# Linear attention and SwiGLU, forward and backward on one core: the key sum on another engine, and loads, stores and transposes around the attention loop at other times

## The chip, the cores and the metric

The kernel runs on one core of a Trainium2 chip. The core has five engines with queues of their own: TensorE (PE in the profile; its weight loads are PEld) multiplies matrices into PSUM, VectorE (DVE) and ScalarE (ACT) work on elements, GpSimd (POOL) does small vector work and issues DMAs, SyncE (SP) issues DMAs. ScalarE's queue can issue DMAs as well. The metric is the device time of one execution in microseconds. Before the change it is 819.78 us, the median of three runs (819.05 to 819.99). The change is measured against that kernel on the same chip.

## The reference

One pre-LayerNorm block with linear attention (32 heads of 20) and a SwiGLU FFN, and the gradients of its input and its five weights for a given `grad_out`. S = 2048 rows, D = 640, F = 1728, everything in bf16.

```python
phi = lambda t: jnp.where(t > 0, t + 1, jnp.exp(t)) + 1e-6
pq, pk = phi(q), phi(k)
kv = jnp.einsum("bhsd,bhse->bhde", pk, v)
z = jnp.einsum("bhsd->bhd", pk)                       # the sum of phi(k) over the rows
num = jnp.einsum("bhqd,bhde->bhqe", pq, kv)
den = jnp.einsum("bhqd,bhd->bhq", pq, z)[..., None] + 1e-6
o = num / den
attn = o.transpose(0, 2, 1, 3).reshape(B, S, D) @ wo

h  = x + attn(layernorm(x))
h2 = h + (silu(layernorm(h) @ w_gate) * (layernorm(h) @ w_up)) @ w_down
# outputs: h2, and the vector-Jacobian products of grad_out with x, wqkv, wo, w_gate, w_up, w_down
```

## The kernel before

The rows are 16 tiles of 128. The program has stages: LayerNorm and the projections of K and Q with phi; Y = xn^T phi(k) and from it the small matrices KVT and W2 (attention and `wo` folded into one 640 x 640 matrix); the attention loop, which forms h and its normalised form hn tile by tile; the FFN in four groups of columns with its weight gradients; then the rest of the backward pass. The change touches what lies from the end of the projections to the first FFN group.

Six pools matter. Each tag has so many slots, which tiles take one after another as they come free.

```python
psum   = tile_pool(bufs=4, space=PSUM)     # each tile two banks: [P, 2, 512] fp32
big    = tile_pool(bufs=5)                 # [P, 16, 640] bf16 and the like: dh2T, xn, xnT, pk, pqa, then pqsT, dm1, hn, hnT, dh2, ...
strips = tile_pool(bufs=4)                 # x_tm, wqk, wvo, then dm0, tzs, yk, dmst, m_s, dd, ...
wpool  = tile_pool(bufs=2)                 # wdT, wdT3, then the FFN weights wgu
work   = tile_pool(bufs=6)                 # rows: xr, zs, ...
fA: rr (used by phi) ; fpool takes its room when fA is closed
```

Gradient steps that don't depend on the attention ("dm" steps: `grad_out @ w_down^T` for two row tiles and one group of columns, ten matmuls and one copy out of PSUM by ScalarE) are kept in a generator and are put between other matmuls:

```python
def dm_steps():
    for g in (0, 1, 3):                       # 8 steps each; 448, 448 and 384 columns
        for t in range(0, ST, 2):
            ps = mm("ps_dm")
            dm_mm(ps, wdT3 if g == 3 else wdT, t, g)
            nc.scalar.copy(out=dst[:, :, :w], in_=ps[:, :, :w])
            if g == 3:
                nc.scalar.dma_start(out=scr_dm_v[:, t:t + 2, :], in_=dst[:, :, :w])
            yield
def dm(n): ...                                # the next n of the 24 steps
```

The head, the sum z and the stage of Y:

```python
warm(31)                                      # 128-wide matmuls of the identity
ln1_stats(0); ln1_centre(0, ...); copies(0, nc.scalar.copy)   # transposes of xn, copied to xnT
warm(8)
# ... cut: projections of K and Q for 16 tiles, phi(which, tiles) on VectorE ...

def z_sum():                                  # 32 matmuls: the rows of pk summed by a matrix of ones
    ps = mm("ps_z")
    for ci, (n0, n1) in enumerate(NCH):       # NCH = two halves of 320 columns
        for t in range(ST):
            q = t % 4 * H
            nc.tensor.matmul(ps[q:q + H, ci, :320], lhsT=ones[:, :H], rhs=pk[:, t, n0:n1],
                             start=(t < 4), stop=(t >= ST - 4))
    nc.scalar.copy(out=half(zs[0][:]), in_=row(ps))                 # z as a bf16 value and a bf16 rest
    nc.vector.tensor_tensor(out=half(zs[1][:]), in0=row(ps), in1=half(zs[0][:]), op=ALU.subtract)
    nc.vector.memset(KVT, 0.0)

for i in range(DT):                           # DT = 5
    ps = mm("ps_y")
    for ci, (n0, n1) in enumerate(NCH):
        for t in range(ST):
            nc.tensor.matmul(ps[:, ci, :320], lhsT=xn[:, t, i * P:(i + 1) * P], rhs=pk[:, t, n0:n1], ...)
        if (i, ci) == (0, 0):
            z_sum()
    nc.scalar.copy(out=half(Yt[:, i, :]), in_=row(ps))
    if i == 0:                                # z broadcast to all partitions: four matmuls ps_zb
        ps_z = mm("ps_zb")
        mm_row(ps_z, lambda k: ones32[:], lambda k, n0, n1: zs[k][:, n0:n1], 2)
        nc.scalar.copy(out=half(zb[:]), in_=row(ps_z))
        masks()
    if 0 < i < 4:
        dm(1)
dm(1)
for t in (0, 4):
    normalise(t)                              # four tiles of phi(q) divided by their denominators, on VectorE
    tr_pqs(t)                                 # their transposes by DMA, on SyncE's queue
# ... cut: kv_blocks (KVT, masked on VectorE), W2T and its transposes W2, with four dm steps between ...
for t in (8, 12):
    normalise(t)
    tr_pqs(t)
dm(2)
```

The attention loop, and the beginning of the FFN:

```python
for t in range(ST + 2):
    if t < ST:
        xr = xrs.pop(t)
        ps = mm("ps_a")
        mm_row(ps, lambda i: pqsT[:, i, t * P:(t + 1) * P], lambda i, n0, n1: W2[:, i, n0:n1], DT)
        nc.vector.tensor_tensor(out=half(xr[:]), in0=row(ps), in1=half(xr[:]), op=ALU.add)   # h1
        ln_stats(xr[:], mv[:, 0, :]); ln_rstd(mv, rstd2, t, 1)        # VectorE, then GpSimd
        dm(1)
    if t > 2:
        load_xr(t + 3)
    u = t - 2
    # ... cut ...
    nc.scalar.dma_start(out=scr_h1_v[:, u, :], in_=h1[:])
    nc.vector.tensor_scalar(out=hn[:, u, :], ...)
    nc.sync.dma_start_transpose(out=hnT[:, :, u * P:(u + 1) * P], in_=hn[:, u, :])

for c in range(4):
    nc.gpsimd.dma_start(out=dh2[:, c * 4:(c + 1) * 4, :], in_=go_v[...])      # the gradient
wgu = {0: load_wgu(0), 1: load_wgu(1)}
for g in range(4):
    for t in range(0, ST, 2):
        # pg and pu: twenty matmuls of hnT and wgu; g == 2 forms its dm step here (pdm)
        nc.scalar.activation(out=dg, in_=pg[:, :, :w], func=ACT.Sigmoid)
        # one more sigmoid and two copies on ScalarE, then seven products and sums on VectorE (m_s, dd);
        # dd transposed by DMA to stg, stg and m_s stored
    # dw: ps_dw from (dh2, m_s) and from (hn, dd), 16 row tiles each; the first one takes
    # the first 14 row tiles of both its parts ahead of the last two
```

Of the kernel before, what the change touches and what calls it, by code (L numbers as in the profile page):

```python
# [8 lines left out]
FP32 = mybir.dt.float32  # L9
# [6 lines left out]
P = 128  # L16
H = 32
# [3 lines left out]
def kernel(  # L21
# [216 lines left out]
    ones32 = const.tile([P, P], BF16, name="ones32")  # L238
    nc.vector.memset(ones32[:], 1.0 / H)
# [70 lines left out]
    def phi(which, t, n=2):  # L310
        e = (pk, pqa)[which][:, t:t + n, :]
        nc.vector.tensor_scalar(out=e, in0=e, scalar1=1.0, scalar2=1e-6, op0=ALU.min, op1=ALU.add)
        nc.vector.tensor_tensor(out=e, in0=e, in1=rr[:, 2 * which + t // 2 % 2, t % 2:t % 2 + n, :], op=ALU.add)
        if (t + n) % 4 == 0:
            sl = slice(t + n - 4, t + n)
            if which == 0:
                nc.sync.dma_start(out=scr_pk_v[:, sl, :], in_=pk[:, sl, :])
            else:
                nc.sync.dma_start(out=scr_pq_v[:, sl, :], in_=pqa[:, sl, :])
                nc.sync.dma_start(out=scr_xnT[sl].rearrange("t p k c -> p t k c"), in_=xnT[:, sl])  # L320

    PIECES = ((0, 3), (3, DT))

    with tc.manual_schedule(engines={EngineType.PE, EngineType.DVE, EngineType.Activation, EngineType.Pool}):
# [16 lines left out]
        warm(31)  # L341
# [16 lines left out]
        for t in range(2, ST):  # L358
# [14 lines left out]
            elif t == ST - 1:  # L373
                phi(0, t, 1)
                phi(1, t - 3)
                phi(1, t - 1)
# [8 lines left out]

    fA.close()
    fpool = wB.enter_context(tc.tile_pool(name="fpool", bufs=6))
# [33 lines left out]
    def masks():  # L421
        tc.keep_in_program_order(nc.gpsimd.memset(mask[:], 1.0))
        for c0, n, p0 in ((0, 6, 0), (120, 2, 88)):
            m = mask[:, c0:c0 + n * Dh]
            for sign in (1, -1):
                tc.keep_in_program_order(nc.gpsimd.affine_select(
                    out=m, in_=m, pattern=[[-sign * Dh, n], [0, Dh]], compare_op=ALU.is_ge, fill=0.0,
                    base=-p0 if sign > 0 else p0 + Dh - 1, channel_multiplier=sign))
# [10 lines left out]
    def normalise(t):  # L439
# [7 lines left out]
        nc.vector.reciprocal(out=rall[:, t:t + 4, :], in_=den[:])  # L447
        nc.vector.tensor_tensor(out=hb4(pq), in0=hb4(pq), in1=bc4(rall[:, t:t + 4, :]), op=ALU.mult)

    def tr_pqs(t):  # L450
        for tt in range(t, t + 4):
# [9 lines left out]
    with tc.manual_schedule(engines={EngineType.PE, EngineType.DVE, EngineType.SP}):  # L461
        yk = strips.tile([P, DT * D + HG * P], BF16, name="yk", tag="S")
        Yt = yk[:, :DT * D].rearrange("p (k n) -> p k n", k=DT)
        KVT = yk[:, DT * D:].rearrange("p (j c) -> p j c", j=HG)
        zs = [wk("zs"), wk("zl")]

        def z_sum():
            ps = mm("ps_z")
            for ci, (n0, n1) in enumerate(NCH):
                for t in range(ST):  # L470
                    q = t % 4 * H
                    nc.tensor.matmul(ps[q:q + H, ci, :320], lhsT=ones[:, :H], rhs=pk[:, t, n0:n1],
                                     start=(t < 4), stop=(t >= ST - 4))
            nc.scalar.copy(out=half(zs[0][:]), in_=row(ps))
            nc.vector.tensor_tensor(out=half(zs[1][:]), in0=row(ps), in1=half(zs[0][:]), op=ALU.subtract)
            nc.vector.memset(KVT, 0.0)

        for i in range(DT):
            ps = mm("ps_y")
            for ci, (n0, n1) in enumerate(NCH):  # L480
# [3 lines left out]
                if (i, ci) == (0, 0):  # L484
                    z_sum()
            nc.scalar.copy(out=half(Yt[:, i, :]), in_=row(ps))
            if i == 0:
                ps_z = mm("ps_zb")
                mm_row(ps_z, lambda k: ones32[:], lambda k, n0, n1: zs[k][:, n0:n1], 2)
                nc.scalar.copy(out=half(zb[:]), in_=row(ps_z))  # L490
                masks()
# [3 lines left out]
        for t in (0, 4):  # L495
            normalise(t)
            tr_pqs(t)
# [14 lines left out]

        kv_blocks(KVT, "ps_kvt", lambda i, a, b: wv[:, i, a:b], lambda i, a, b: Yt[:, i, a:b])

# [3 lines left out]
        for i in range(DT):  # L518
# [5 lines left out]
            nc.sync.dma_start_transpose(out=W2[:, :, i * P:(i + 1) * P], in_=W2T[:, i, :])  # L524
        for t in (8, 12):
            normalise(t)
            tr_pqs(t)
        dm(2)

        hn = big.tile([P, ST, D], BF16, name="hn", tag="B")  # L530
        hnT = big.tile([P, DT, S], BF16, name="hnT", tag="B")
        h1s = {}
        for t in range(ST + 2):
# [10 lines left out]
            if t > 2:  # L544
                load_xr(t + 3)
# [488 lines left out]
```

## Time and profile before

| What | us |
|---|---|
| Median of three runs (lowest, highest) | 819.78 (819.05, 819.99) |
| Span of the profiled execution, first to last instruction | 817.2 |
| First matmul of Y (ps_y) | 54.6 |
| First matmul of the attention loop (ps_a) | 98.1 |
| First matmul of the FFN (pg) | 146.4 |
| First matmul of its first weight gradient (ps_dw) | 176.7 |
| Last matmul ends | 813.8 |

Granted TensorE clock over the span: 1.000. The first column of a line in the order of time is the start in microseconds from the first instruction, the second its length or, for several of a kind, the length of the stretch; then come the engine, the line of the program, the operation, output and inputs, and a count. An entry in brackets is time for which the engine stood idle before it, and what ended the wait. Matmuls overlap, and the profile models their ends: what one costs in a row is seen from start to start. ScalarE's queue (ACTq) and SyncE's queue (SPq) show the issue of DMAs, not the transfers.

### The profile page before, as it was taken

What the parts mean: (1) busy time and instruction counts of PE and PEld (TensorE: products, weight loads), DVE (VectorE), ACT (ScalarE), POOL (GpSimd) and SP (SyncE); (2) the same over time, 40 slices, a digit from 0 to 9 for tenths busy, and PEclk for the clock granted to TensorE, in tenths of its full rate; (3) what the DMA queues carried; (4) which work ended last, traced back from release to release, by engine and by line L of the source; (5) the groups of instructions that cost most, each with busy time, mean ns of one, the idle gap of its engine ahead of it and who ended that gap; (6) DMA issues with size and microseconds to landing.
All of it is one profiled execution on the core that took longest, in us unless ns stands there. A gap on an engine that the chain in (4) does not pass through costs nothing.

```text
span 817.2 us, 13969 instructions
## 1 busy us (share of the span) xinstructions
PE 811.2 (99%) x5534; PEld 521.7 (64%) x5534; DVE 442.5 (54%) x849; ACT 288.2 (35%) x405; POOL 192.8 (24%) x350
## 2 busy tenths in 40 slices
PE   9999999999999999999999999999999999999998
PEld 7776666545555555555566677777777777777675
DVE  7878787791087018800760147787892366631212
ACT  6982422760184126400841122322312133322010
POOL 3420022223312412221125501211220121112330
PEclk9999999999999999999999999999999999999999
DMA  9994789999559987993498757976499999999942
GB/s 302 192 360 86 169 202 277 258 221 214 132 137 222 205 201 153 206 268 81 107 252 165 259 134 219 216 213 167 114 239 165 175 159 181 174 212 251 273 132 72
DMA packets 278321, 158.61 MB, mean 194 GB/s; under 512 B 235052, under 2 KB 264877, under 8 KB 278256
## 3 DMA queue, kind: packets, MB, share of 16 engines
q1 hardware_dynamic: 251696, 82.12, 52.7%
q0 software_dynamic: 17744, 64.45, 26.0%
q10 hardware_dynamic: 8816, 11.16, 4.5%
q8 instruction: 43, 0.70, 0.4%
q14 instruction: 22, 0.18, 0.1%
HBM read 47.68 MB, written 53.66 MB: 124 GB/s over the span
## 4 chain that ended last, share of the span: by engine, by line
PE 94%; DVE 4%; DMA 1%; ACT 0%; issue 0%; ACTq 0%; DVEq 0%
PE ps_dw L652 21%; PE ps_dhn L109 14%; PE ps_dxn L904 8%; PE ps_o L966 7%; PE ps_kq L302 5%; PE ps_dwqk L109 5%; PE pg L583 5%; PE pu L588 5%; PE ps_dm L396 5%; PE ps_y L482 3%; PE ps_gt L711 3%; PE ps_dp L109 3%; PE ps_dk L109 3%; PE ps_a L109 3%; PE pdm L396 2%; DVE m_s L613 1%
## 5 line engine op out<-in xcount | busy, mean ns | idle before, releaser
L109 PE MATMUL ps_dhn<-wgT,cols 128*128 128x320 bf16 x864 | 119.5, 299 | 0.0
L652 PE MATMUL ps_dw<-dd,hn 128*128 128x448 bf16 (+1 forms) x640 | 118.8, 346 | 0.0
L109 PEld LDWEIGHTS <-cols 128*128 128x128 bf16 x864 | 84.5, 98 | 32.9
L652 PEld LDWEIGHTS <-hn 128*128 128x128 bf16 x640 | 62.6, 98 | 54.2
L654 DVE CAST dwev<-ps_dw 128x896 bf16<-128x896 f32 (+3 forms) x12 | 10.9, 906 | 122.9 <-PE ps_dw L652 122.9
L654 ACT CAST dwev<-ps_dw 128x896 bf16<-128x896 f32 (+1 forms) x20 | 17.6, 878 | 159.4 <-PE ps_dw L652 151.5
L617 POOL DMA_DIRECT2D scr_dT<-stg x64 | 34.7, 542 | 164.2 <-DMA stg<-dd 159.4
L147 DVE CUSTOM_DVE_ANT_0 lb_a<-lb_dy,hn 128x640 bf16<-128x640 bf16 x32 | 26.5, 829 | 75.5 <-ACT lb_dy L145 75.5
L583 PE MATMUL pg<-wgu,hnT 128*128 128x448 bf16 (+1 forms) x320 | 63.6, 346 | 0.0
L588 PE MATMUL pu<-wgu,hnT 128*128 128x448 bf16 (+1 forms) x320 | 63.6, 346 | 0.0
L652 PE MATMUL ps_dw<-m_s,dh 128*128 128x448 bf16 (+1 forms) x320 | 60.7, 346 | 0.6 <-DVE m_s L613 0.4
L966 PE MATMUL ps_o<-wd,mT 128*128 128x320 bf16 (+3 forms) x462 | 61.1, 295 | 0.0
L904 PEld LDWEIGHTS <-ring 128*128 128x128 bf16 x480 | 47.0, 98 | 18.2
L966 PEld LDWEIGHTS <-mT 128*128 128x128 bf16 (+1 forms) x462 | 41.8, 97 | 17.4 <-issue 2.6
L904 PE MATMUL ps_dxn<-wqkvT,ring 128*128 128x320 bf16 x320 | 51.3, 299 | 0.0
L652 PEld LDWEIGHTS <-dh 128*128 128x128 bf16 x320 | 31.3, 98 | 28.0 <-issue 1.1
L588 PEld LDWEIGHTS <-hnT 128*128 128x128 bf16 x320 | 31.3, 98 | 27.1
L583 PEld LDWEIGHTS <-hnT 128*128 128x128 bf16 x320 | 31.3, 98 | 27.0
L396 PE MATMUL ps_dm<-wdT,dh2T 128*128 128x448 bf16 (+1 forms) x240 | 47.0, 344 | 0.0
L396 PEld LDWEIGHTS <-dh2T 128*128 128x128 bf16 x320 | 31.0, 98 | 24.8
L302 PE MATMUL ps_kq<-wqk,xnT 128*128 128x320 bf16 x320 | 46.3, 299 | 0.0
L145 ACT ACTIVATE lb_dy<-ps_dhn,rstd 128x640 bf16<-128x640 f32 x16 | 12.7, 793 | 87.1 <-PE ps_dhn L109 87.1
(166 smaller groups left out, 1277.4 us busy)
## 6 DMA issues: line engine op xcount, KB each, us to landing
scr_dT<-stg POOLq DMA_DIRECT2D x48, 224.0 KB, 3.2
cols<-scr_dT POOLq DMA_DIRECT2D x6, 1728.0 KB, 8.3
scr_m<-m_s POOLq DMA_DIRECT2D x12, 448.0 KB, 4.5
cols<-scr_dT ACTq DMA_DIRECT2D x2, 1728.0 KB, 10.2
out_dram<-dwev POOLq DMA_DIRECT2D x30, 112.0 KB, 2.2
scr_dT<-stg POOLq DMA_DIRECT2D x16, 192.0 KB, 2.9
scr_pk<-pk SPq DMA_DIRECT2D x4, 640.0 KB, 8.2
scr_xnT<-xnT SPq DMA_DIRECT2D x4, 640.0 KB, 8.2
```

What stands on the lines that cost most here:

```text
L109: nc.tensor.matmul(ps[:, ci, :320], lhsT=lhs(k), rhs=rhs(k, *NCH[ci]), start=(start and k == 0), stop=(stop and k == n - 1))
L147: nc.vector.tensor_tensor_reduce(out=a[:], in0=dy[:], in1=xhat, scale=1.0, scalar=0.0, op0=ALU.mult, op1=ALU.add, accum_out=sums[:, 1:2])
L302: nc.tensor.matmul(ps[:, ci, :320], lhsT=xnT[:, t, k, :], rhs=wqk[:, k, w0 + n0:w0 + n1], start=(k == 0), stop=(k == DT - 1))
L396: nc.tensor.matmul(ps[:, c, :w], lhsT=dh2T[:, kt, (t + c) * P:(t + c + 1) * P], rhs=wdT[:, kt, o:o + w], start=(kt == 0), stop=(kt == DT - 1))
L482: nc.tensor.matmul(ps[:, ci, :320], lhsT=xn[:, t, i * P:(i + 1) * P], rhs=pk[:, t, n0:n1], start=(t == 0), stop=(t == ST - 1))
L583: nc.tensor.matmul(pg[:, c, :w], lhsT=hnT[:, kt, (t + c) * P:(t + c + 1) * P], rhs=wg[:, kt, 0:w], start=(kt == 0), stop=(kt == DT - 1))
L588: nc.tensor.matmul(pu[:, c, :w], lhsT=hnT[:, kt, (t + c) * P:(t + c + 1) * P], rhs=wg[:, kt, w:2 * w], start=(kt == 0), stop=(kt == DT - 1))
L617: nc.gpsimd.dma_start(out=scr_dT[t + c, :, KO[g]:KO[g] + GK[g], :], in_=stg[:, :GK[g], :])
L652: nc.tensor.matmul(ps[:, c, :w], lhsT=lhs(t), rhs=rhs(t), start=(t == 0), stop=(t == ST - 1))
L654: last = copy(out=ev[:, :len(parts), :w], in_=ps[:, :len(parts), :w])
L904: nc.tensor.matmul(ps[:, ci, :320], lhsT=lhs[:, i, :], rhs=rhs[:, i, n0:n1], start=(k == 0 and i == 0), stop=(k == 2 and i == DT - 1))
L966: nc.tensor.matmul(po(t, ci), lhsT=mTs[t // 4][r, t % 4, j, :], rhs=wd[r, j, n0:n1], start=(t, ci) not in opened, stop=last)
```

## The change

It does several things at once between the projections and the FFN. z is summed by VectorE in fp32 rather than by matmuls with ones, ahead of the last four tiles of phi(q); only its broadcast stays on TensorE, later in the stage. Twelve of the 24 dm steps come ahead of the attention loop, where nine did; one of the others stands inside the first row of the loop. Transposes of the last normalised tiles and of hn are spread over the loop, h1 is stored through GpSimd's queue instead of ScalarE's, and a one-column sigmoid in the loop makes ScalarE load its table there. The gradient and the second FFN weights are loaded only after the first sigmoid of the second pair of tiles of the first FFN group. The aim is to take work off TensorE and to have the other engines' queues free where the FFN begins. The diff, with cuts:

```diff
-    ones32 = const.tile([P, P], BF16, name="ones32")
-    nc.vector.memset(ones32[:], 1.0 / H)
...
-        warm(31)
+        warm(37)
...
             elif t == ST - 1:
-                phi(0, t, 1)
-                phi(1, t - 3)
-                phi(1, t - 1)
+                last_phi = phi(0, t, 1)
...
-    def normalise(t):
+    def norm_den(t):
... (the first four operations) ...
+    def norm_mul(t):
... (the product) ...
-    with tc.manual_schedule(engines={EngineType.PE, EngineType.DVE, EngineType.SP}):
+    with tc.manual_schedule(engines={EngineType.PE, EngineType.DVE, EngineType.SP, EngineType.Pool}):
+        z2 = tzs[:, 4:8].rearrange("p t d -> p (t d)").bitcast(FP32)
+        zf = z2[:, :D]
+        tok2 = pk.rearrange("p (t two) d -> p t (two d)", two=2)
+        with tc.issue_after(last_phi):
+            nc.vector.tensor_tensor(out=z2, in0=tok2[:, 0], in1=tok2[:, 1], op=ALU.add)
+        for t in range(2, ST // 2):
+            nc.vector.tensor_tensor(out=z2, in0=z2, in1=tok2[:, t], op=ALU.add)
+        nc.vector.tensor_tensor(out=zf, in0=zf, in1=z2[:, D:], op=ALU.add)
         zs = [wk("zs"), wk("zl")]
-        def z_sum(): ... (whole, as shown above)
+        nc.vector.tensor_copy(out=zs[0][:], in_=zf)
+        nc.vector.tensor_tensor(out=zs[1][:], in0=zf, in1=zs[0][:], op=ALU.subtract)
+        for t in (ST - 4, ST - 2):
+            phi(1, t)
+        nc.vector.memset(KVT, 0.0)
+        masks()
+        def z_bcast():
+            ps = mm("ps_zb")
+            mm_row(ps, lambda k: ones[:], lambda k, n0, n1: zs[k][:, n0:n1], 2)
+            nc.scalar.copy(out=half(zb[:]), in_=row(ps))
...
-                if (i, ci) == (0, 0):
-                    z_sum()
+                if (i, ci) == (2, 1):
+                    z_bcast()
... (ps_zb after i == 0 is gone) ...
-        for t in (0, 4):
-            normalise(t)
-            tr_pqs(t)
+        norm_den(0)
+        norm_mul(0)
+        tr_pqs(0)
+        norm_den(4)
...
         kv_blocks(KVT, "ps_kvt", ...)
+        norm_mul(4)
...
+        tr_pqs(4)
         for t in (8, 12):
-            normalise(t)
-            tr_pqs(t)
-        dm(2)
+            norm_den(t)
+            norm_mul(t)
+            if t < 12:
+                tr_pqs(t)
+        dm(5)
...
-                mm_row(ps, lambda i: pqsT[...], lambda i, n0, n1: W2[:, i, n0:n1], DT)
+                for ci, (n0, n1) in enumerate(NCH):
+                    for i in range(DT):
+                        nc.tensor.matmul(ps[:, ci, :320], lhsT=pqsT[...], rhs=W2[:, i, n0:n1], ...)
+                    if t == 0 and ci == 0:
+                        dm(1)
...
-                dm(1)
+                if t > 0 and t % 4 != 3:
+                    dm(1)
+            while h1_todo and h1_todo[0][0] < t:
+                v, h1 = h1_todo.pop(0)
+                nc.gpsimd.dma_start(out=scr_h1_v[:, v, :], in_=h1[:])
             if t > 2:
                 load_xr(t + 3)
+            if t < 4:
+                tr_pqs(12 + t, 1)
+            if t == 3:
+                hnT = big.tile([P, DT, S], BF16, name="hnT", tag="B")
...
             if u == 0:
+                nc.scalar.activation(out=small.tile([P, 1], FP32, ...)[:], in_=h1s[0][1][:, 0, 0:1], func=ACT.Sigmoid)
...
-            nc.scalar.dma_start(out=scr_h1_v[:, u, :], in_=h1[:])
...
-            nc.sync.dma_start_transpose(out=hnT[:, :, u * P:(u + 1) * P], in_=hn[:, u, :])
+            hnT_todo.append(u)
+            for v in hnT_todo[:0 if t < 4 else 2]:
+                hnT_todo.pop(0)
+                nc.sync.dma_start_transpose(out=hnT[:, :, v * P:(v + 1) * P], in_=hn[:, v, :])
+    fA.close()                                   # moved here from ahead of the stage of Y
+    fpool = wB.enter_context(tc.tile_pool(name="fpool", bufs=6))
...
-        wgu = {0: load_wgu(0), 1: load_wgu(1)}
+        wgu = {0: load_wgu(0)}                   # and the four loads of dh2 became the generator load_dh2()
...
+                sig = nc.scalar.activation(out=dg, in_=pg[:, :, :w], func=ACT.Sigmoid)
+                if g == 0 and t == 2:
+                    wait_for(sig, load_dh2())
+                    wgu[1] = load_wgu(1)
```

## The prediction

> **What bounds the kernel now.** I read the page's busy table first, then the groups, then the order of time on TensorE and the chain that ended last, stage by stage. From the page:
>
> ```profile
> PE 811.2 (99%) x5534; PEld 521.7 (64%) x5534; DVE 442.5 (54%) x849; ACT 288.2 (35%) x405; POOL 192.8 (24%) x350
> ```
>
> TensorE is busy for 811.2 of 817.2 us. Matmul ends are modelled, so a busy share alone doesn't say that it runs at full rate; spacings do. In the view in order of time, ten 448-wide matmuls take 1.89 us (189 ns from start to start) and ten 320-wide take 1.36 us (136 ns), and these spacings hold almost everywhere. So TensorE is the bound, and only two things shorten the kernel: fewer matmuls, or the few places where its spacing breaks. From the groups, kept apart by shape, the matmuls that this change removes:
>
> ```profile
> L472 PE MATMUL ps_z<-pk,ones 128*32 128x320 bf16 x32 | 1.3, 300 | 0.0
> ```
>
> And from the order of time around the end of the K and Q projections, the first break (start, length, engine, line, count):
>
> ```profile
> 94.33 3.94 PE L396 MATMUL ps_dm<-wdT,dh2T 128*128 128x448 bf16 x20
> ...
> 98.11 0.84 PE L109 MATMUL ps_a<-wvo,pqsT 128*128 128x320 bf16 x5
> ...
> 99.14 0.85 PE L109 MATMUL ps_a<-wvo,pqsT 128*128 128x320 bf16 x5 [0.19 <-DMA wvo<-wvo]
> ```
>
> Five 320-wide matmuls from 98.11 end their issue at 98.11 + 5 x 0.136 = 98.79, the next start at 99.14: 0.35 us lost to the last transpose of W2. The second break is at the first dw of the FFN, from TensorE's order of time:
>
> ```profile
> 176.71 2.43 PE L652 MATMUL ps_dw<-m_s,dh 128*128 128x448 bf16 x12
> 179.56 4.25 PE L652 MATMUL ps_dw<-m_s,dh 128*128 128x448 bf16 x20 [0.42 <-DVE m_s L613]
> 183.65 6.59 PE L652 MATMUL ps_dw<-dd,hn 128*128 128x448 bf16 x34
> ```
>
> 176.71 + 12 x 0.189 = 178.98, so 0.58 lost before 179.56; 179.56 + 20 x 0.189 = 183.34, so 0.31 lost before 183.65. Both times VectorE hadn't written m_s. Why it was late is read from the chain that ended last (start, length, what):
>
> ```profile
> 149.31 0.16 ACTq L554
> 149.48 0.03 issue
> 149.51 1.28 ACT L604
> 150.80 0.92 ACT dd L604
> ...
> 153.36 0.64 DVE m_s L613
> ...
> 182.23 0.62 DVE m_s L613
> 182.86 0.04 issue
> 182.90 7.16 PE ps_dw L652 x37
> ```
>
> ScalarE's queue was held by the last h1 stores (L554) until 149.48, then it loaded the sigmoid table, 1.28 us, and VectorE could begin only at 153.36. In this stage VectorE needs about as long for a pair of tiles (seven products of 0.54 us, 3.8 us) as TensorE (two times 1.89 us), so it never makes up a late start. A last gap lies at the head: 31 warm-up matmuls from 1.42, 107 ns apart, end at 4.73, and the transposes start at 5.35. All breaks after the head together are about 2 us of 817, so the change has little room.
>
> [...]here spacings fall from 107 to 56 ns at about 6.5 us. [...]the trace before has none from SBUF, but its fp32 add out of PSUM (xr, 640 elements) takes 818 ns[...]; the group of L604 shows the same 1283 ns.
>
> **The change part by part.**
>
> z on VectorE. It removes the 32 ones-matmuls: in the chain they stand for 1.20 us (56.92 to 58.12), and the sixteen ps_y matmuls right after them take 2.28 instead of 2.17 us. Saved on the path: 1.3 us. Added on VectorE after the last phi of K (ends 55.5): seven fp32 adds of 1280 elements,[...] one of 640 (0.82), a cast of 640 (about 0.5) and a difference (0.82). With about 30 ns between dependent operations that is 12.9 us, an estimate, so the two z halves stand at 68.4. The broadcast (4 matmuls, 0.54 us, as before) now comes after the third ps_y row: 54.74 + 3 x 4.35 + 1.89 = 69.7. It should not wait, with 1.3 us to spare.
>
> VectorE afterwards. The last two phi of Q (2.6 us) and the memset (0.4) follow, to 71.4; zb is ready at about 71.5, where it was 61.75. Each group of four tiles costs 1.49 + 2.82 + 0.23 + 0.95 = 5.5 us for the denominators and 2.83 for the product, 8.4 with gaps. First group to 79.9, second denominators to 85.5. TensorE reaches ps_kvt at 84.6 and ends it at 86.0 (a dm step of 1.89 follows), the masks are done at 86.9: no wait. Three more products and two denominators end at about 106.6, where it was 104.5.
>
> Twelve dm steps ahead. They were nine, so the loop starts 3 x 1.9 - 1.3 = 4.4 us later, at 98.1 + 4.4 = 102.5. W2's transposes landed at 99.1 before, so the 0.35 us break goes. Moved steps cost nothing: all 24 remain. The first ps_a row ends at about 105.8 (0.68 + 1.9 + 0.68, as a dm step now stands in its middle) and VectorE picks it up at 106.6; four PSUM buffers cover that. In the loop TensorE needs (4 x 1.36 + 3 x 1.62)/4 = 2.6 us per tile with the narrow steps, VectorE 0.82 + 0.89 + 0.21 + 0.40 plus gaps, 2.45. It holds, narrowly.
>
> h1 stores on GpSimd, table early. ScalarE's queue is free of the sixteen stores and has its table since about 108. TensorE starts the FFN at 146.44 - 1.3 - 0.35 = 144.8, the first pg is complete 2.1 us later, and ScalarE starts at about 147.0 instead of 150.80. VectorE starts 2.56 us after that, at about 149.5 instead of 153.36: 3.8 us earlier, while TensorE is 1.65 us earlier. The slack of 2.2 us exceeds the 0.89 us lost at the first dw, so both waits go.
>
> Loads and transposes. The gradient load and the second weight pair start after the third sigmoid at about 151, and so leave the queue to the hn transposes. They were issued at 145 to 151 and land in some 10 us; the first dw needs the gradient at 175. Hidden before and after.
>
> Head. Six more warm-up matmuls fill the 0.62 us gap, but nothing gets ready sooner: the transposes wait for xn. The order of the built program also puts the mask's memset (the identity's memset of 128 columns takes 0.20 us there, this one has 160) ahead of the identity; then 37 x 0.107 from about 1.6 ends at 5.55, 0.2 later than now.[...] I book +0.1.
>
> Sum: -1.3 - 0.35 - 0.89 + 0.1 = -2.4 us, so 819.8 - 2.4 = 817.4.
>
> **The rivals.**
> 1. VectorE becomes the bound between 55 and 110. For it: 12.9 us of new work where it had 1.2, on an engine that the loop uses to 94%. Against: it stood idle for 7.7 us ahead of the kvt masks, which the new work may fill. If the adds cost 20% more, z is late by about 1 us and TensorE waits for zb or the masks: 818 to 819. If the loop falls behind as well, the FFN start loses what the table gave: 820.
> 2. The later loads are missed. The fourth gradient piece stands in GpSimd's queue behind two stores of transposed tiles, which wait for SyncE's transposes; those stood back until 163 before. If that repeats, the piece is issued at about 167 and, at up to 10 us to landing, comes by 177, just when it is needed (175 + 12 x 0.19). A miss costs 1 to 5 us: 818 to 822.
> 3. The m_s waits stay, because something else than the table holds ScalarE (the slot of dd, a store). Then 0.9 is not won: 818.3.
>
> **Range and chances.** The sum is three small terms, each read off to about 0.1 us; the three runs before spread over 0.94 us. Rival 3 and the head give a high side of about 1 us, rivals 1 and 2 (together perhaps one in six) up to 3 more. An earlier clock is the only gain beyond the sum. I predict 817.4 us, with 816.3 to 819.2 for 8 in 10. Two per cent are 16.4 us, far more than any break can return or any rival costs: faster 0.01, within 2% 0.98, slower 0.01.
>
> **What would show it.** Right: no ps_z; 50 ps_dm matmuls back to back ahead of ps_a with no DMA wait; ps_dw of the first group without an m_s wait; first m_s product at about 149.5; TensorE's first pg at about 144.8; zl ready ahead of ps_zb. Wrong: ps_zb or ps_kvt's masks waiting for VectorE, ps_dw waiting for a DMA of dh, pg for hnT, or a first kq later than 6.9. A time above 819.5 would refute the sum, one below 816 would mean that I overlooked a loss.

## The result, and the profile after

The changed kernel takes 822.36 us (median of 6 runs, 821.62 to 822.93); the kernel before, in the same measurements, 819.67 (818.49 to 820.91). The ratio is 1.0032 with a 95% interval of 1.0019 to 1.0045: the change costs 2.7 us, where the prediction had it win 2.4. The gains that the prediction listed did come. A new wait in the attention loop, with a stretch of half clock behind it, took more than all of them.

From the page of the kernel after, the busy table and the costliest group that now waits (busy, mean ns | idle before, releaser). The 32 ones-matmuls of z are gone and six warm-up matmuls are new (5508 instead of 5534), yet TensorE's busy time is longer (812.0 for 811.2 us), which points to matmuls that ran slower:

```profile
PE 812.0 (99%) x5508; PEld 522.5 (64%) x5508; DVE 453.0 (55%) x857; ACT 288.1 (35%) x405; POOL 200.4 (24%) x366
...
L390 PE MATMUL ps_dm<-wdT,dh2T 128*128 128x448 bf16 (+1 forms) x240 | 47.5, 348 | 3.2 <-DVE xr L549 3.2
```

TensorE in order of time, kernel after (start, length, engine, line, count, idle time before it and its releaser):

```profile
93.33 9.62 PE L390 MATMUL ps_dm<-wdT,dh2T 128*128 128x448 bf16 x50
102.79 0.84 PE L545 MATMUL ps_a<-wvo,pqsT 128*128 128x320 bf16 x5
103.47 2.05 PE L390 MATMUL ps_dm<-wdT,dh2T 128*128 128x448 bf16 x10
...
133.42 2.88 PE L545 MATMUL ps_a<-wvo,pqsT 128*128 128x320 bf16 x20
139.47 2.73 PE L390 MATMUL ps_dm<-wdT,dh2T 128*128 128x384 bf16 x10 [3.17 <-DVE xr L549]
142.00 2.30 PE L545 MATMUL ps_a<-wvo,pqsT 128*128 128x320 bf16 x10
144.13 1.79 PE L390 MATMUL ps_dm<-wdT,dh2T 128*128 128x384 bf16 x10
...
150.10 2.06 PE L612 MATMUL pg<-wgu,hnT 128*128 128x448 bf16 x10
...
180.37 2.43 PE L684 MATMUL ps_dw<-m_s,dh 128*128 128x448 bf16 x12
183.22 3.96 PE L684 MATMUL ps_dw<-m_s,dh 128*128 128x448 bf16 x20 [0.42 <-DMA dh<-in_grad_out_dram]
```

The reader sees three of the announced signs: fifty dm matmuls in a row, no wait for W2 at the first ps_a (102.79 + 5 x 0.136 = 103.47), no wait for m_s at ps_dw. And two that were named as signs of being wrong: 3.17 us of idle TensorE at 139.47, after which ten 384-wide matmuls take 2.73 us instead of 1.79, and a wait of ps_dw for the gradient (180.37 + 12 x 0.189 = 182.64, so 0.58 lost). The first pg comes at 150.10; it was announced for 144.8.

Two windows of 5 us from the same trace (length, then busy time of TensorE, its weight loads, VectorE, ScalarE and GpSimd, granted clock, DMA share, GB/s). From 140.16 on the clock is at half for 3.41 us:

```profile
135.00:140.00 5.00, 1.83 (x14) 1.13 (x13) 1.37 (x3) 0.80 (x1) 0.00 (x0) 1.00 0.99 245
140.00:145.00 5.00, 5.00 (x24) 2.77 (x23) 4.83 (x13) 0.80 (x1) 2.92 (x6) 0.66 0.99 289
```

What VectorE waited for, from its order of time:

```profile
130.91 0.82 DVE L549 TENSOR_TENSOR xr<-ps_a,xr 128x640 bf16<-128x640 f32 x1 [1.73 <-DMA xr<-in_A_x_dram]
...
138.59 0.82 DVE L549 TENSOR_TENSOR xr<-ps_a,xr 128x640 bf16<-128x640 f32 x1 [5.38 <-DMA xr<-in_A_x_dram]
```

It is the load of x (xr) of tile 10, the residual that is added to the attention's row. Until it lands, the PSUM buffers aren't freed and TensorE stops. The chain of waits of the kernel after, at this place, names the load as the longest piece:

```profile
130.63 7.84 DMA xr<-in_A_x_dram
...
138.59 0.84 DVE xr L549
139.43 0.04 issue
139.47 2.73 PE ps_dm L390 x10
```

Why it came so late shows in SyncE's queue, which issues one transfer after another. Kernel after (start, issue time, line, count):

```profile
98.34 15.37 SPq L449 DMA_TRANSPOSE pqsT<-pqa  x11
...
126.45 0.52 SPq L456 DMA_DIRECT2D xr<-in_A_x_dram  x1
127.07 0.61 SPq L185 DMA_DIRECT2D wgu<-in_B_w_gate_dram  x1
127.73 0.74 SPq L186 DMA_DIRECT2D wgu<-in_B_w_up_dram  x1
128.56 1.98 SPq L581 DMA_TRANSPOSE hnT<-hn  x1
130.63 0.86 SPq L456 DMA_DIRECT2D xr<-in_A_x_dram  x1
```

and the same queue of the kernel before, where the load of tile 10 is the one at 123.94:

```profile
97.75 13.00 SPq L452 DMA_TRANSPOSE pqsT<-pqa  x8
...
122.21 0.38 SPq L185 DMA_DIRECT2D wgu<-in_B_w_gate_dram  x1
122.69 1.21 SPq L557 DMA_TRANSPOSE hnT<-hn  x1
123.94 0.56 SPq L459 DMA_DIRECT2D xr<-in_A_x_dram  x1
124.56 0.48 SPq L186 DMA_DIRECT2D wgu<-in_B_w_up_dram  x1
```

The queue differs in three ways. As z comes later, normalise does, and twelve pqsT transposes instead of eight stand behind W2's, at 1.2 us of issue or more each. The loop's hnT transposes start late and then come two a step. And both wgu loads of the first FFN group (0.56 MB each), which the diff doesn't touch, now stand together, just in front of tile 10's load. It is issued 6.7 us later than before and takes 7.84 us to land instead of 4.6, while VectorE wants it only 1.5 us later (133.21 for 131.73). The twelve transposes aren't what puts the two halves of wgu there: with z left on TensorE eight stand behind W2's, and the halves fall together all the same (below, the rest alone).

Had the kernel before shown this risk? Yes. In its loop the transfer engines are as full (DMA share 1.15 from 125 to 140), and its tile 11 was already late, only not by enough to reach TensorE. VectorE of the kernel before:

```profile
134.99 0.82 DVE L538 TENSOR_TENSOR xr<-ps_a,xr 128x640 bf16<-128x640 f32 x1 [0.96 <-DMA xr<-in_A_x_dram]
```

That load had taken 7.80 us from issue to landing, behind the second wgu load.

### The profile page after: what moved, and what is told of

Read it like the earlier page. It is cut to its first block, busy times and chain, and to the rows that moved or that the text cites. A ratio compares the mean times of both kernels' runs of the same rounds, so it can differ in the third digit from the quotient of the medians.

```text
span 820.0 us, 13924 instructions
## 1 busy us (share of the span) xinstructions
PE 812.0 (99%) x5508; PEld 522.5 (64%) x5508; DVE 453.0 (55%) x857; ACT 288.1 (35%) x405; POOL 200.4 (24%) x366
## 4 chain that ended last, share of the span: by engine, by line
PE 94%; DMA 4%; DVE 1%; issue 0%; ACT 0%; SPq 0%; POOL 0%; DVEq 0%; POOLq 0%
PE ps_dw L684 21%; PE ps_dhn L109 14%; PE ps_dxn L936 8%; PE ps_o L998 7%; PE pg L612 6%; PE ps_kq L300 5%; PE ps_dwqk L109 5%; PE pu L617 5%; PE ps_dm L390 5%; PE ps_dk L109 3%; PE ps_gt L743 3%; PE ps_dp L109 3%; PE ps_y L487 3%; PE ps_a L545 2%; PE pdm L390 2%; DMA stg<-dd 2%
```

## The experiments

The theories: A, the xr loads are late because they stand in SyncE's queue behind the transposes (issue). B, they are late because the wgu loads in front of them hold up their transfer (landing). C, the h1 stores by GpSimd disturb. D, VectorE is too slow for the loop. F, the transfer engines are full whatever they carry. All times are compared with runs of the kernel before on the same chip (819.2 to 819.4 us). The changed kernel itself was timed beside a median of 819.67, so a difference from its 822.36 is good to about half a microsecond. A trace is one execution of its kernel: where a run's times spread over several microseconds, others of its executions went differently.

**wgu behind all xr loads, and in the middle.** Both edits make the first group's two loads wait for a later hn (`after=hn[11]` is shorthand for a dependency of both loads on the VectorE instruction that writes hn of tile 11):

```diff
-        wgu = {0: load_wgu(0)}
+        wgu = {0: load_wgu(0, after=hn[11])}   # e2_wgu_late: behind the xr load of tile 15
+        wgu = {0: load_wgu(0, after=hn[6])}    # e5_wgu_mid: behind the xr load of tile 12
```

> The two loads wgu of the first FFN group wait for hn of tile 11, so that they stand behind all xr loads in SyncE's queue; everything else stands as in the changed kernel. Theory B: xr of tile 10 lands 3.4 us after its issue as its neighbours do, instead of 7.84; with its issue at about 129.3 (1.35 us of two issues less ahead of it) it is there at 132.7, about when VectorE wants it, so the stall of 5.4 us falls below 0.5 us and the time to about 817.4 to 818. Theory A in its pure form: only the 1.35 us of issue is won, the landing stays long because the transposes remain, stall about 4 us, 820 to 821. The wgu loads themselves land by about 150 and could add up to 2 us of wait at the first pg matmul, seen there and not at the xr adds.

Measured: 824.02 us, ratio 1.0056 (1.0044 to 1.0068). Tile 10's load, issued at 128.84, landed in 5.52 us; TensorE lost nothing over 0.25 us in the loop. The cost moved to the first pg, as the load of wgu, issued at 144.74, was on the path itself, and half clock came there too (6.83 us from 147.96 on). The 817.4 to 818 expected for B didn't come. TensorE of this run:

```profile
143.48 1.52 PE L547 MATMUL ps_a<-wvo,pqsT 128*128 128x320 bf16 x10
150.55 3.89 PE L616 MATMUL pg<-wgu,hnT 128*128 128x448 bf16 x10 [5.55 <-DMA wgu<-in_B_w_gate_dram]
```

So the loop's stall depends on where wgu stands, and the place has a limit on the other side as well. VectorE kept up with the loop here (TensorE waited for none of its adds), which rules out D.

> The first FFN group's two wgu loads wait for hn of tile 6 and so stand behind the xr load of tile 12 in SyncE's queue: four loads later than in the changed kernel, and about 8 us earlier than in the run that put them behind all xr loads. If those 1.1 MB in front of the xr loads of tiles 10 to 12 make the loop's stall (theory B with A), the loop is as in that run: no idle TensorE over 0.3 us in it, no half clock; and wgu, issued near 135, lands by 144, ahead of the first pg, which then starts at about 145.5: 822.4 - 5.0 = 817.4 us (816.8 to 818.3). If something else makes it (the queue's order, the full transfer engines whatever they carry), 1 to 3 us of stall stay, 819 to 822.

Measured: 816.13 us (815.5 to 816.33), ratio 0.9959 (0.9946 to 0.9971): 3.1 us faster than the kernel before, and some 6 us below the changed kernel's 822.36. SyncE's queue of this run:

```profile
128.05 0.61 SPq L458 DMA_DIRECT2D xr<-in_A_x_dram  x1
...
132.62 0.52 SPq L458 DMA_DIRECT2D xr<-in_A_x_dram  x1
133.23 0.38 SPq L185 DMA_DIRECT2D wgu<-in_B_w_gate_dram  x1
...
135.84 0.46 SPq L186 DMA_DIRECT2D wgu<-in_B_w_up_dram  x1
```

and its TensorE, without a break from the loop to the first dw's end:

```profile
143.14 1.52 PE L547 MATMUL ps_a<-wvo,pqsT 128*128 128x320 bf16 x10
144.50 2.05 PE L616 MATMUL pg<-wgu,hnT 128*128 128x448 bf16 x10
...
174.77 6.22 PE L688 MATMUL ps_dw<-m_s,dh 128*128 128x448 bf16 x32
180.82 5.46 PE L688 MATMUL ps_dw<-dd,hn 128*128 128x448 bf16 x28
```

The first pg at 144.50 is what the prediction had (144.8), and all 32 matmuls of the first dw follow each other (174.77 + 32 x 0.189 = 180.82). Here the gains of the prediction's sum pay at once.

**The same move on the kernel before (control).**

```diff
-        wgu = {0: load_wgu(0), 1: load_wgu(1)}
+        wgu = {0: load_wgu(0, after=hn[6]), 1: load_wgu(1)}
```

> The control: the kernel before, with wgu of the first group behind the xr load of tile 12 as well, nothing else of the change. Its loop has no stall of TensorE to lose (one wait of VectorE for xr of tile 11, 0.96 us, hidden), so if the 6 us won by that move were the change's own new wait, here it is worth nothing: 819.2 us (818.6 to 819.8; up to 1 more if wgu then lands behind the first pg). If the move is a gain of its own, 816 to 818.

Measured: 819.34 us, ratio 1.0000 (0.9992 to 1.0008). The move is worth nothing by itself; it only takes away what the change had put in.

**Other traffic taken out of the loop.** The stores of W2T and KVT are issued by ScalarE ahead of the loop. So that wgu and xr keep their order, wgu waits for hn of tile 3:

```diff
-                nc.sync.dma_start(out=scr_KVT..., in_=KVT)       # in the loop, step 2
-                nc.sync.dma_start(out=mat_v(scr_W2T), in_=W2T)   # in the loop, step 4
+        act_load(scr_KVT..., KVT)                                # ahead of the loop
+        act_load(mat_v(scr_W2T), W2T)
...
-        wgu = {0: load_wgu(0)}
+        wgu = {0: load_wgu(0, after=hn[3])}
```

> The changed kernel with the stores of W2T and KVT (0.8 and 0.19 MB) taken from SyncE's queue inside the loop and issued by ScalarE ahead of the loop, where the transfer engines are busy 0.6 of the time; wgu and all xr loads keep their order in SyncE's queue. Theory F (the transfer engines are full in the loop): some 3 us of their work leave the stretch before tile 10's load, so its landing or its issue comes 2 to 3 us earlier, the idle stretch of TensorE shrinks from 3.2 us to below 1.5 and the half clock goes: 818 to 819.5 us. Theory A by issue alone: 1.0 us less of issue in SyncE's queue, tile 10 one us earlier, idle 2.2 us, no half clock: 819.5 to 820. Theory B (wgu right in front of tile 10's load makes the whole wait): no change, 821.5 to 822.5.

Measured: 821.40 us, ratio 1.0022 (1.0008 to 1.0035). The chain of waits of this run:

```profile
128.54 10.29 DMA xr<-in_A_x_dram
...
138.95 0.83 DVE xr L553
```

Tile 10's load was issued 2.1 us earlier than in the changed kernel, as A has it, and landed at 138.83 instead of 138.47: the whole gain of issue was lost in the landing. This is B's answer, and it speaks against F in the form that any megabyte less would help. It doesn't exclude it: 6 of the 22 executions of this run kept the full clock and took 817.59 to 818.94 us, so there the load was probably less late. From the issues and landings in the traces, one execution each, for tile 10's load:

| kernel | stands ahead of it | issued | landed | took |
|---|---|---|---|---|
| before | first half of wgu | 123.94 | 128.56 | 4.62 |
| after | both halves of wgu | 130.63 | 138.47 | 7.84 |
| W2T, KVT early | both halves | 128.54 | 138.83 | 10.29 |
| h1 stores on ScalarE | both halves | 129.72 | 135.99 | 6.27 |
| rest alone | both halves | 131.90 | 138.32 | 6.41 |
| 48 matmuls, second try | both halves | 131.85 | 139.26 | 7.40 |
| transposes not spread | second half | 131.63 | 137.69 | 6.06 |
| wgu late | (behind all xr) | 128.84 | 134.36 | 5.52 |
| wgu in the middle | (behind tile 12) | 128.05 | 133.13 | 5.08 |
| five more runs with wgu moved | (behind tile 12) | 123.94 to 130.42 | 126.62 to 134.07 | 2.67 to 5.15 |

With both halves of wgu in front it takes 6.3 to 10.3 us and lands between 136.0 and 139.3, and the earliest issue (128.54) doesn't bring it in earliest; with none in front it takes 2.7 to 5.5 us.

**xr from another queue.**

```diff
-            nc.sync.dma_start(out=xrs[t][:], in_=x_v[:, t, :])
+            nc.sync.dma_start(...) if t < 6 else act_load(...)   # e1_xr_act; act_load: by ScalarE, in program order
+            (nc.sync if t < 6 else nc.gpsimd).dma_start(...)     # e6_xr_pool
```

> The ten xr loads of tiles 6 to 15 are issued by ScalarE's queue instead of SyncE's; nothing else changes. Theory A (the loads are late because they stand in SyncE's in-order queue behind the transposes): tile 10 is issued about as early as its buffer comes free, some 6 us earlier than 130.63, VectorE's waits for xr (7.1 us in two) are gone, TensorE's 3.2 us idle before the dm step at 139.47 is gone, and with it the stretch of half clock; 822.4 - 5.0 = 817.4 us (816.6 to 818.2). Theory B (the loads are late because they share the transfer engines with the two wgu loads of 0.57 MB each): the landing of the load behind wgu stays near 7 to 8 us and leaves at least 1.5 us of stall; 819 to 821 us. Theory D (VectorE is too slow for the loop by itself): no change, 821.5 to 822.5.

> The xr loads of tiles 6 to 15 are issued by GpSimd, behind the h1 store of the tile before, instead of SyncE. GpSimd waits in the loop only for the rows' rstd, so tile 10 is issued near 127 instead of 130.6 (its buffer comes free when the h1 store of tile 4 lands, about 126). Theory A (place in SyncE's queue): loads there by 132, stall below 0.5 us, 817.0 to 818.2. Theory F (all transfer engines are full from 105 to 150, so whatever is issued after 122 takes 5 to 8 us): issue 3.5 us earlier, landing 5 to 7: the stall falls to about 1 to 2 us[...], 818 to 819.5.

Measured: 821.26 us, ratio 1.0023 (1.0014 to 1.0033), from ScalarE; 823.55, ratio 1.0050 (1.0034 to 1.0065), from GpSimd. Neither is A's 817. On ScalarE the loads were not even issued earlier: tile 9's came at 129.54 instead of 126.45, because that queue stood behind its own dm copies and stores. On GpSimd tile 10's came at 127.73, 2.9 us earlier, as expected, and took 7.63 us to land, though no wgu stood in that queue (7.84 from SyncE's). The GpSimd run's profiled execution was 5.5 us faster than its median, so only its issue and landing times are used here.

**The h1 stores back on ScalarE**, in the changed kernel and with wgu in the middle:

```diff
-                nc.gpsimd.dma_start(out=scr_h1_v[:, v, :], in_=h1[:])
+            nc.scalar.dma_start(out=scr_h1_v[:, u, :], in_=h1[:])
```

> The stores of h1 go back from GpSimd's queue to ScalarE's, after hn as in the kernel before. Theory C[...]: the stall is gone, 817 to 818.5 us. Theories A and B: SyncE's queue is as it was, so tile 10 is still issued near 130.6 and VectorE waits about 5 us for it, the half clock follows, and the time stays 821.5 to 823 us (the two m_s waits do not depend on this edit's queue and stay away).

> The run with wgu behind the xr load of tile 12, and the h1 stores on ScalarE's queue again. If the h1 stores by GpSimd cost time only by freeing xr buffers later, which shows only while the loop stalls, nothing is left to win: 816.1 us (815.6 to 816.6), VectorE's two waits for xr (0.9 and 1.3 us) shorter. If GpSimd's stores cost by themselves[...], 815.0 to 815.5. If they were a help for the loop (ScalarE's queue held up dm copies), 816.5 to 818.

Measured: 818.68 us, ratio 0.9993 (0.9986 to 1.0000), and 819.63, ratio 0.9998 (0.9986 to 1.0010). The same edit wins 3.7 us on the changed kernel and loses 3.5 on the one with wgu moved, so C isn't a cost of its own. In the first, tile 10 landed 2.5 us earlier, TensorE lost 2.05 us instead of 3.33, there for a dm copy of ScalarE, and no half clock followed (in 18 of its 21 executions); which of the queues brought the load forward stays open. In the second the loss can be read. ScalarE of that run:

```profile
138.46 4.57 ACTq L576 DMA_DIRECT2D scr_h<-xr  x2
143.06 0.80 ACT L406 CAST dmst<-ps_dm 128x768 bf16<-128x768 f32 x1 [6.52 <-DMA wgu<-in_B_w_up_dram]
```

and its TensorE:

```profile
143.91 1.78 PE L392 MATMUL ps_dm<-wdT,dh2T 128*128 128x384 bf16 x10 [1.91 <-ACT dmst L406]
```

Two h1 stores held ScalarE's queue for 4.57 us, and the dm copy behind them freed its PSUM buffer too late. Their own issue takes 0.35 and 0.33 us of it. For 3.8 us between them the queue waited for the second half of wgu, which SyncE had issued and which landed at 142.63; the second store is issued 0.06 us later. The store has no data in common with wgu. In the trace of the kernel before, where the same shows, the two have a semaphore in common: ScalarE's queue waits for 3.55 us from 129.09 on for the semaphore on which wgu's second half signals, the last signal comes at 132.61, and at 132.68 the h1 store is issued, which signals its landing on the same one. So a large load can hold a queue that doesn't carry it. In the second run another 1.35 us was lost to the gradient's last piece. The move of these stores to GpSimd is worth having once the loads are in order.

**The spread of the transposes undone.**

```diff
-            if t < 12:
-                tr_pqs(t)
+            tr_pqs(t)                       # all sixteen ahead of the loop, hnT one a step
```

> The spread of the transposes is undone: the last four pqsT transposes stand ahead of the loop again, and hnT follows one a step from tile 0 on, without the catch-up of two a step. Theory A, by the number of transposes (twelve pqsT instead of eight behind W2's, as normalise comes later): the queue is as full as before the edit, the xr loads of tiles 6 and 7 move to about 116 to 118, the later ones come about 1 to 2 us earlier than in the changed kernel; part of the stall stays, 818.5 to 821 us. Theory A, by the catch-up alone: the stall goes, 817 to 818 us. Theory B: one wgu load stands between two xr loads at a time, as in the kernel before, and the landing falls to about 4 to 5 us, so most of the stall goes too, 817.5 to 818.5.

Measured: 818.95 us, ratio 0.9998 (0.9989 to 1.0006). The two halves of wgu stand apart again (126.34 and 128.87). VectorE now waits for five xr loads, 0.90 to 2.19 us each, together 7.8, and TensorE loses 0.77 and 1.78 us; no half clock followed, in 13 of 14 executions. The spread with its catch-up of two hnT a step is therefore a part of the cause, through where it lets wgu fall, but not all of it.

**The half clock.** 48 matmuls that nobody needs, placed into the idle stretch; the first try put them behind the tile's add in the program, the second ahead of it:

```diff
+                if t == 12:
+                    for _ in range(48):
+                        nc.tensor.matmul(ps[:, 0, 320:320 + P], lhsT=ident[:], rhs=ident[:], start=True, stop=True)
```

> The changed kernel with 48 matmuls of 128x128 more, whose results nobody reads, between ps_a of tile 12 and the dm step that stood idle for 3.17 us. They take about 2.7 us at full clock and fit into that idle time. If the 3.4 us at half clock that follow the stall are caused by the idle stretch, the stall of VectorE stays (about 5 us, waiting for tile 10's xr), the granted clock stays 1.00 and pg starts 1.7 us earlier than at 150.1: 820.5 to 821.2 us in place of 822.4. If the half clock has another cause, it stays, and the time is 822 to 823.

> The changed kernel with 48 matmuls of 128x128 more, whose results nobody reads, right behind ps_a of tile 12 and now ahead of that tile's VectorE add in the program, so that they wait for nothing and run in the 3.17 us in which TensorE stood idle (in the earlier try they waited for the add and made the idle stretch 7.5 us). If the half clock after the stall comes from the idle stretch, VectorE's wait for tile 10's xr stays near 5 us, the clock stays at 1.00 behind it, and the time is 822.4 - 1.7 = 820.7 us (820.2 to 821.3). If the half clock has another cause, it stays: 822 to 823.

Measured: the first, 828.23 us, ratio 1.0107 (1.0088 to 1.0126). Its matmuls waited for the add of their own tile, TensorE stood for 7.34 us, and 6.83 us of half clock followed; it didn't test the theory. The second, 819.72 us, ratio 1.0003 (0.9995 to 1.0011): more matmuls, and 2.6 us less than the changed kernel. Two windows of its trace, columns as above:

```profile
135.00:140.00 5.00, 4.18 (x60) 3.68 (x58) 0.62 (x1) 0.80 (x1) 0.00 (x0) 1.00 0.88 197
140.00:145.00 5.00, 4.75 (x32) 3.03 (x32) 4.83 (x12) 0.80 (x1) 2.70 (x6) 1.00 1.12 302
```

VectorE's wait for tile 10 was even longer (6.89 us), but TensorE stood idle for only 1.08 us of it and the clock stayed at 1.00, in this and in all other executions of that kernel. So the idle stretch makes the half clock. All six executions of the changed kernel had it, with a mean clock of 0.996 or 0.998 (0.998 fits one stretch of 3.41 us in 820, 0.996 two); four had 0.996, and the profiled one 0.998.

**One part alone, and with wgu in the middle.**

```diff
 e7_z_alone:    z's adds, phi, normalise and masks of the change; the loop, the h1 stores and the FFN loads of before
 e8_rest_alone: the loop, the h1 stores, the table and the FFN loads of the change; z and normalise of before
 e15_z_mid, e16_rest_mid: the same two, with load_wgu(0, after=hn[6])
```

> The kernel before with one part of the change alone: z summed by VectorE (with normalise and the pqsT transposes as late as that makes them, and the longer warm-up); dm steps, h1 stores, hnT and FFN loads as before. If z's late normalise is what fills SyncE's queue behind W2 (twelve pqsT transposes instead of eight), xr loads come 3 to 5 us later than in the kernel before and tiles 8 to 11 stall VectorE by 1 to 4 us: 819 to 822 us in place of 819.4 - 1.3 + 0.3 = 818.4. If the loss comes from the other parts, 818.0 to 818.7.

> Everything of the change but z: z stays with TensorE as before, so normalise of tiles 0 to 7 and eight pqsT transposes are done by 84 us, and eight instead of twelve stand behind W2's. If z's late normalise is the cause, SyncE is 4 to 5 us further on at the loop, no stall: 819.4 - 0.35 - 0.89 = 818.1 us (817.7 to 818.8). If the spread with its catch-up of two hnT a step is the cause by itself, tile 10's load is again behind wgu and two hnT, the stall of 3 us and the half clock stay: 820.5 to 823.

> The kernel before with z summed by VectorE alone, and wgu of the first group behind the xr load of tile 12. If wgu in front of the xr loads is also what made z alone slower (idle TensorE of 1.69 and 1.39 us in its loop), those two go and the wait for W2 at the first ps_a (1.6 us) stays: 821.5 - 3.0 = 818.5 us (817.8 to 819.2). If the twelve pqsT transposes by themselves make xr late, 820 to 821.5.

> Everything of the change but z, and wgu behind the xr load of tile 12. The loop's stall (2.1 us and, in part of the runs, the half clock) goes, and what is left is the two booked gains, 0.35 + 0.89 us: 819.2 - 1.2 = 818.0 us (817.4 to 818.6). Together with the run of z alone this says whether the parts' gains add up to the 3.1 us of the whole change with wgu moved.

| | as the kernel has it | wgu in the middle |
|---|---|---|
| nothing of the change | 819.2 to 819.4 | 819.34 |
| z alone | 821.49, ratio 1.0025 (1.0018 to 1.0033) | 820.91, ratio 1.0021 (1.0013 to 1.0029) |
| the rest alone | 819.36, ratio 1.0009 (0.9996 to 1.0022) | 818.70, ratio 0.9990 (0.9978 to 1.0002) |
| both (the change) | 822.36, ratio 1.0032 (1.0019 to 1.0045) | 816.13, ratio 0.9959 (0.9946 to 0.9971) |

With wgu in the middle the parts don't add up: beside their kernel before, z alone costs 1.5 us and the rest alone wins 0.7, both together win 3.1. They need each other. TensorE of z alone shows where its 1.3 us went:

```profile
99.00 0.85 PE L109 MATMUL ps_a<-wvo,pqsT 128*128 128x320 bf16 x5 [1.43 <-DMA wvo<-wvo]
...
133.18 1.79 PE L390 MATMUL ps_dm<-wdT,dh2T 128*128 128x384 bf16 x10 [1.53 <-ACT dmst L404]
137.56 1.79 PE L390 MATMUL ps_dm<-wdT,dh2T 128*128 128x384 bf16 x10 [1.23 <-ACT dmst L404]
```

TensorE came to the first ps_a earlier and waited there for W2, 1.6 us lost instead of 0.35; the two later waits are for ScalarE's dm copies. In front of each stands an h1 store that was issued only when a half of wgu had landed (131.84 and 136.28), as above. In the change twelve dm steps cover the first wait, and the h1 stores aren't in ScalarE's queue. Moving wgu did not cure z alone: 820.91, where 818.5 was expected. TensorE lost 1.83 us for W2 there, and 1.00 and 1.06 for dm copies that again stood behind h1 stores (one waited for wgu's second half, 141.75). The xr load of tile 6 stands behind all twelve pqsT transposes and lands at 122.80, after VectorE had been idle for 4.0 us: issue order, theory A, holds for that load, though TensorE lost nothing by it.

The rest alone leaves z on TensorE and shows what puts the two halves of wgu together. SyncE's queue of its profiled execution (820.98 us):

```profile
129.01 0.41 SPq L185 DMA_DIRECT2D wgu<-in_B_w_gate_dram  x1
129.46 0.52 SPq L186 DMA_DIRECT2D wgu<-in_B_w_up_dram  x1
130.08 1.73 SPq L574 DMA_TRANSPOSE hnT<-hn  x1
131.90 0.72 SPq L456 DMA_DIRECT2D xr<-in_A_x_dram  x1
```

That is the order of the changed kernel, with eight pqsT transposes behind W2's instead of twelve; TensorE stood idle for 1.97 us, and half clock followed. In z alone (127.21 and 129.65) and in the run without the spread the halves stand apart. So the spread of the transposes puts them together, not z's delay. The median of the rest alone hides this: 7 of its 21 executions had half clock and took 820.98 to 824.5 us.

The rest alone with wgu moved missed 818.0 by 0.7: in its trace the m_s waits at ps_dw are back (0.66 and 0.31 us), with the table load early all the same. Its first m_s product comes 6.5 us after the first pg (152.49 against 145.98); in the run with both parts and wgu in the middle it is 4.7. VectorE came late from the loop there: it waited 1.52 and 1.70 us for xr of tiles 13 and 14, and its add of tile 15 began at 149.01 instead of 145.69.

**The head undone**, with wgu in the middle:

```diff
-        warm(37)
+        warm(31)
-        nc.gpsimd.memset(mask[:], 1.0)
+        tc.keep_in_program_order(nc.gpsimd.memset(mask[:], 1.0))
... (the mask's affine_select in the same way)
```

> The run with wgu behind the xr load of tile 12 (816.1 us), and the head undone on top: 31 warm matmuls instead of 37, the mask's memset behind the identity's. The head was booked at +0.3 us by the first transposes (first kq at 6.86 instead of 6.63), so 815.8 us (815.4 to 816.2) if it is on the path[...].

Measured: 816.29 us, ratio 0.9969 (0.9960 to 0.9977), so nothing won. The warm matmuls started at 1.42 instead of 1.55, but 0.54 us of m_s waits came back at ps_dw. VectorE had waited 1.83 us for xr of tile 14 in the loop there (1.30 with the head as changed), so they needn't come from the head. Whether the head is worth 0.1 or 0.3 us can't be told from this.

## Why the prediction was wrong

The step that failed is the one on the loop: "In the loop TensorE needs (4 x 1.36 + 3 x 1.62)/4 = 2.6 us per tile with the narrow steps, VectorE 0.82 + 0.89 + 0.21 + 0.40 plus gaps, 2.45. It holds, narrowly." It set two engines against each other and left out the third thing a tile needs, its xr load. SyncE's queue, which carries it, appears nowhere in the sum, and neither do the wgu loads, whose place the change moves without naming them. The part of the change that moves them, the spread of the transposes, has no line in the prediction's list of parts. Rival 1 looked for a stall in this stage, but by VectorE's own work. The term missing from the sum is 5.0 us in the profiled execution: 3.3 of idle TensorE and 1.7 of half clock.

| step of the prediction | said | the runs showed |
|---|---|---|
| z removed from TensorE | -1.3, z halves at 68.4 | right: VectorE's work takes 12.9 us as estimated (55.74 to 68.63; the first add of 1280 elements 1.48, the six after it 9.12, the one of 640 0.83), so zl ends at 68.6; the ps_y stage is 28.1 instead of 29.4 us |
| dm steps fill the wait for W2 | -0.35, loop from 102.5 | right: 102.79, no wait |
| table early, both m_s waits go | -0.89 | right after the change (table load at 106.48, 1.28 us; before, 149.51); not by the table alone: they are back, 0.97 and 0.54 us, where VectorE comes late from waits for xr (the rest alone with wgu moved, the head undone) |
| first m_s product | 4.7 us behind the first pg | right: 154.75 against 150.10 |
| head | +0.1 | 0.3 later at the first ps_y (54.89 for 54.58), but from one profiled execution with 37 warm-up matmuls to the next that start varies from 54.30 to 55.17; no gain measured when undone |
| loop holds, narrowly | 0 | wrong: +5.0 |
| later loads "Hidden before and after" | 0 | wrong in size: +0.58, the gradient's last piece, as rival 2 described it |

With these, -1.3 - 0.35 - 0.89 + 0.3 + 0.6 + 5.0 = +3.4 us, and the last matmul ends 3.36 later (817.20 for 813.84). With wgu moved behind tile 12 the missing term is gone and the kernel is 3.1 us faster than before, a little more than the -2.4 that was booked. In the profiled execution of that run the last matmul ends 2.84 us earlier than before (811.00 for 813.84); 0.28 of it is a first ps_y at 54.30, where full clock was granted at about 4.4 (an estimate: 26 warm-up matmuls from 2.70 on took 2.42 us there, and in the traces of before and after they are 107 ns apart ahead of full clock and 56 behind it) instead of 6.48. In the profiled execution of the changed kernel, with 37 warm-up matmuls as well, it was granted at 7.04.

## What to carry to other kernels

When a change delays the work that feeds a queue of transfers, write down the queue's order before and after, with the issue time of each, and follow every load that something waits for: a large load that nobody wants yet can fall in front of a small one that is wanted now, without a line of it being in the diff. A load that lands just as it is needed is a wait that hasn't happened yet; look for it in the kernel before. And price a stall of TensorE with the half clock that may follow it: here 3.3 us of idle time were followed by 3.41 us of it, which cost another 1.7.

## What the hardware showed

The half clock came in stretches of 3.41 us, or twice that (6.83 with wgu behind all xr loads and in the first try with 48 matmuls). The clock's record in the two traces of before and after has more such lengths. In the changed kernel the clock was full for 133.120 us from 7.04 on, at half for 3.413, and full again for 675.839; in the kernel before it was full for 812.372 from 6.48 on. These are 39, 1, 198 and 238 times 3.4133 us.

How long TensorE must stand isn't fixed: 2.68 us of idle time (the profile with xr from ScalarE) brought no half clock, 1.97 us (the profile of the rest alone) brought 3.41 us of it from 139.50 on. So the length of a wait doesn't decide it alone; what else does, and where the limit lies, isn't shown. Executions of one kernel differ in it as well: 7 of 21 of the rest alone had the half clock, 14 had not.

In the changed kernel the two halves of wgu (0.56 MB each) had landed by 136.06, tile 10's 0.16 MB, issued behind them, only at 138.47. The ten xr loads of the loop took 2.6 to 7.8 us to land in the kernel before and 2.5 to 7.8 in the changed one; tile 10's took 10.29 with W2T and KVT stored early.
